# A new order for the first batch, four queries to a partition, and stores on ScalarE's queue in an attention-and-MLP kernel

## The chip, the cores and the metric

The kernel runs on one core of one Trainium2 chip. The metric is device time in microseconds (us), lower is better. Engines are named as in the profile: PE is TensorE's matmul, PEld its weight load, DVE is VectorE, ACT is ScalarE, POOL is GpSimd, SP is SyncE, which here only issues DMAs. A name with a q behind it (SPq, ACTq) is that engine's instruction sequencer, for instance when it issues a DMA. PSUM is the memory in which PE leaves its products. "L494" is line 494 of the kernel that is being profiled.

## The reference

Eight batches of causal retention (attention without softmax, with a decay by distance), followed by a low-rank mix of tokens and an MLP, both with a residual. Inputs and outputs are float32.

```python
# q, k, v: (8 batches, 8 heads, 576 tokens, 64)
scores = q @ k^T / sqrt(64)
ret    = scores * where(i >= j, gamma[h] ** (i - j), 0)
x      = concat_heads(ret @ v)                       # (8, 576, 512)
h      = (x^T @ U @ V)^T                             # U: (576, 32), V: (32, 576)
u      = x + h
out    = u + relu(u @ w_ch1) @ w_ch2                 # w: (512, 2048), (2048, 512)
```

## The kernel before

A batch has 4.5 chunks of 128 tokens, so two batches share nine chunks, the fifth being half one batch's and half the other's. The work on one batch before its MLP is called its front: load, cast, transpose q and k (`TQ`, `TK` in the new kernel), scores (`SC`), the masked scores `ret` on DVE, values (`RV`), the scaled result `xt` on DVE, the mix (`MA`, `MH`) that gives `ut`, and `uT`. The MLP has two halves, `Y1` (ACT evicts with Relu) and `Y2` (DVE adds the residual into `o_sb`, which is stored). From batch 1 on, the front of the next batch is interleaved with the MLP of the current one.

```python
def load_chunk(p, c):                                # one chunk: q, k, v together
    t = qkv_pool.tile([P, 3, H, D], BF16, ...)
    f = stage.tile([P, 3, H, D], FP32, ...)
    for j, dram in ((1, k), (0, q), (2, v)):
        for rows, b, t0 in parts(p, c):
            nc.sync.dma_start(out=f[rows, j, :, :],  # partition = token, 256-byte pieces
                in_=dram[b, :, t0:t0 + L, :].rearrange("h s d -> s h d"))
    nc.vector.tensor_copy(out=t[:, 0:2, :, :], in_=f[:, 0:2, :, :])      # DVE: cast q, k
    nc.gpsimd.tensor_tensor(out=t[:, 2, :, :], in0=f[:, 2, :, :], ...)   # POOL: cast, scale v
# ... Y2, its last step: one store of 128 rows in order, on SP
    nc.vector.tensor_tensor(out=o_sb, in0=ps, in1=st["u", c0 + i], op=ALU.add)
    nc.sync.dma_start(out=out_flat[row0 + i * P:row0 + (i + 1) * P, :], in_=o_sb)
# ... the program: only PE, POOL and SP are in manual order, DVE and ACT are not
with tc.manual_schedule(engines={PE, POOL, SPQ}):
    ...
    interleave([], front_items(0, [], True, 0))
    load_w1(range(1, dff // W1B)); load_w2()
    for g in range(2 * NP):
        interleave(mlp_items(...), front_items(g + 1, chunks_of(g + 2)), 0.35 if g == 0 else 0.05, 0.9)
```

Of the kernel before, what the change touches and what calls it, by code (L numbers as in the profile page):

```python
# [9 lines left out]
FP32 = mybir.dt.float32  # L10
# [4 lines left out]
POOL = mybir.EngineType.Pool  # L15
SPQ = mybir.EngineType.SP
# [23 lines left out]
def kernel(  # L40
# [25 lines left out]

    XC = 4
    NCH = 9

# [5 lines left out]
    stage = ctx.enter_context(tc.tile_pool(name="stage", bufs=4))  # L75
    qkv_pool = ctx.enter_context(tc.tile_pool(name="qkv_pool", bufs=9))
    qkT_pool = ctx.enter_context(tc.tile_pool(name="qkT_pool", bufs=6))
# [5 lines left out]
    mix_pool = ctx.enter_context(tc.tile_pool(name="mix_pool", bufs=2))  # L83
# [7 lines left out]


# [3 lines left out]
    pos = consts.tile([P, NCH, H], FP32, name="pos")  # L96
    lngt = consts.tile([P, NCH, H], FP32, name="lngt")
# [3 lines left out]

# [3 lines left out]
    V_B = consts.tile([P, 5 * P], BF16, name="V_B")  # L105

    vx = [consts.tile([P, H, D], BF16, name=f"vx{i}") for i in range(2)]

    qTx = [consts.tile([P, NHP, P], BF16, name=f"qTx{i}") for i in range(2)]
    w1_sb = consts.tile([P, NCC, dff], BF16, name="w1_sb")  # L110
    w2_sb = consts.tile([P, NF, dm], BF16, name="w2_sb")

    def early_consts():
        make_identity(nc, ident)
        nc.gpsimd.memset(lnb, math.log(scale))

        nc.gpsimd.iota(
            pos[:, 0:5, :], pattern=[[P, 5], [0, H]], base=0, channel_multiplier=1,
            allow_small_or_imprecise_dtypes=True,
        )  # L120
        nc.gpsimd.iota(
            pos[:, 5:NCH, :], pattern=[[P, 4], [0, H]], base=P, channel_multiplier=1,
            allow_small_or_imprecise_dtypes=True,
        )
        nc.gpsimd.iota(
            pos[HALF:P, XC, :], pattern=[[0, H]], base=HALF, channel_multiplier=1,
            allow_small_or_imprecise_dtypes=True,
        )
        for h in range(H):
            nc.vector.memset(lngt[:, :, h], lng[h])  # L130
        nc.vector.tensor_tensor(out=lngt, in0=lngt, in1=pos, op=ALU.mult)
        nc.scalar.activation(out=vscale, in_=lngt, func=AF.Exp, bias=lnb, scale=-1.0)
        nc.scalar.activation(out=qscale, in_=lngt, func=AF.Exp, bias=0.0, scale=1.0)
        make_upper_triangular(nc, tri, val=1.0, diag=True)
        nc.vector.tensor_copy(out=trix, in_=tri)
        nc.vector.memset(trix[0:HALF, HALF:P], 0.0)
        for t in vx:
            nc.vector.memset(t[0:HALF, :, :], 0.0)
        for t in qTx:
            nc.vector.memset(t[:, :, HALF:P], 0.0)  # L140
        for t in (U_A, U_B, V_A, V_B):
            nc.vector.memset(t, 0.0)

    def load_mixer():
        nc.gpsimd.dma_start(
            out=U_A[:, 0:4, 0:R],
            in_=moe_U[0:4 * P, :].rearrange("(c p) r -> p c r", p=P),
        )
        nc.gpsimd.dma_start(out=U_A[0:HALF, 4, 0:R], in_=moe_U[4 * P:S, :])
        nc.gpsimd.dma_start(out=V_A[0:R, 0:S], in_=moe_V)  # L150
        nc.gpsimd.dma_start(out=U_B[HALF:P, 0, 0:R], in_=moe_U[0:HALF, :])
        nc.gpsimd.dma_start(
            out=U_B[:, 1:5, 0:R],
            in_=moe_U[HALF:S, :].rearrange("(c p) r -> p c r", p=P),
        )
        nc.gpsimd.dma_start(out=V_B[0:R, HALF:HALF + S], in_=moe_V)

    W1B = 512

    def load_w1(fbs):  # L160
        for fb in fbs:
            for cc in range(NCC):
                nc.gpsimd.dma_start(  # L163
                    out=w1_sb[:, cc, fb * W1B:(fb + 1) * W1B],
                    in_=moe_w_ch1[cc * P:(cc + 1) * P, fb * W1B:(fb + 1) * W1B],
                )

    def load_w2():
        for f in range(0, NF, 2):
            nc.gpsimd.dma_start(  # L170
                out=w2_sb[:, f:f + 2, :],
                in_=moe_w_ch2[f * P:(f + 2) * P, :].rearrange("(f p) d -> p f d", p=P),
            )

    def parts(p, c):

        if c < XC:
            return [(slice(0, P), 2 * p, c * P)]
        if c > XC:
            return [(slice(0, P), 2 * p + 1, c * P - 4 * P - HALF)]  # L180
        return [(slice(0, HALF), 2 * p, 4 * P), (slice(HALF, P), 2 * p + 1, 0)]


    def load_chunk(p, c):
        t = qkv_pool.tile([P, 3, H, D], BF16, tag="qkv", name="qkv")
        f = stage.tile([P, 3, H, D], FP32, tag="stage", name="stage_t")
        for j, dram in ((1, k), (0, q), (2, v)):
            for rows, b, t0 in parts(p, c):
                L = rows.stop - rows.start
                nc.sync.dma_start(  # L190
                    out=f[rows, j, :, :],
                    in_=dram[b, :, t0:t0 + L, :].rearrange("h s d -> s h d"),
                )
        nc.vector.tensor_copy(out=t[:, 0:2, :, :], in_=f[:, 0:2, :, :])  # L194
        nc.gpsimd.tensor_tensor(  # L195
            out=t[:, 2, :, :], in0=f[:, 2, :, :],
            in1=vscale[:, c, :, None].to_broadcast([P, H, D]), op=ALU.mult,
        )
        if c == XC:
            nc.gpsimd.tensor_copy(out=vx[p % 2][HALF:P, :, :], in_=t[HALF:P, 2, :, :])  # L200
        sts[p]["qkv"][c] = t


    def attention_items(p, chunks, st, pe_transpose, lag, loads):
        items = []
        qkv = st["qkv"]
        loads = list(loads)

        def T(c):
            t = qkv[c]  # L210
            qkT = qkT_pool.tile([P, 2 * NHP, P], BF16, tag="qkT", name="qkT")
            st["qkT", c] = qkT
            if not pe_transpose:
                nc.sync.dma_start_transpose(  # L214
                    out=qkT, in_=t[:, 0:2, :, :].rearrange("p j h d -> p (j h d)")
                )
                return
            pst = ps_big.tile([P, 2 * NHP, P], BF16, tag="ps_big", name="pst")
            for j in (1, 0):
                for hp in range(NHP):  # L220
                    nc.tensor.transpose(  # L221
                        pst[:, j * NHP + hp, :],
                        t[:, j, 2 * hp:2 * hp + 2, :].rearrange("p h d -> p (h d)"),
                        ident,
                    )
            nc.scalar.activation(out=qkT, in_=pst, func=AF.Copy)  # L226

        def ST(c):

            t = qkv[c]  # L230
# [4 lines left out]
            vt = vx[p % 2] if c == XC else t[:, 2, :, :]  # L235
            for hp in range(NHP):
                nc.tensor.matmul(  # L237
                    pss[:, hp, :],
                    t[:, 1, 2 * hp:2 * hp + 2, :].rearrange("p h d -> p (h d)"),
                    vt[:, 2 * hp:2 * hp + 2, :].rearrange("p h d -> p (h d)"),  # L240
                    start=(first and hp == 0), stop=True, skip_group_check=True,
                )
# [4 lines left out]
        def SC(c):  # L247

            qkT = st["qkT", c]
            psc = ps_sc.tile([P, 2, NHP, P], FP32, tag="ps_sc", name="psc")  # L250
            for hp in range(NHP):
                for hl in range(2):
                    pb = hl * HALF
                    nc.tensor.matmul(  # L254
                        psc[:, hl, hp, :],
                        qkT[pb:pb + HALF, NHP + hp, :],
                        qkT[pb:pb + HALF, hp, :],
                        start=True, stop=True,
                    )
            po = ps_o.tile([P, 2, 512], FP32, tag="ps_o", name="po")  # L260
            st["po", c] = po
            if c > 0:
                s_sb = st["s", c - 1]
                qT = qkT
                if c == XC:
                    qT = qTx[p % 2]
                    nc.gpsimd.tensor_copy(
                        out=qT[:, :, 0:HALF], in_=qkT[:, 0:NHP, 0:HALF]
                    )
                for hp in range(NHP):  # L270
                    for hl in range(2):
                        pb = hl * HALF
                        nc.tensor.matmul(
                            po[:, hl, hp * D:(hp + 1) * D],
                            qT[pb:pb + HALF, hp, :],
# [3 lines left out]
            ret = ret_pool.tile([P, H, P], BF16, tag="ret", name="ret")  # L279
            mask = trix if c == XC else tri  # L280
            nc.vector.tensor_tensor(  # L281
                out=ret.rearrange("p (hp hl) i -> p hl hp i", hl=2), in0=psc,
                in1=mask[:, None, None, :].to_broadcast([P, 2, NHP, P]),
                op=ALU.mult,
            )
            st["ret", c] = ret

        def RV(c):
            t = qkv[c]
            ret = st["ret", c]  # L290
            po = st["po", c]
            for h in range(H):
                hp, hl = h // 2, h % 2
                nc.tensor.matmul(  # L294
                    po[:, hl, hp * D:(hp + 1) * D], ret[:, h, :], t[:, 2, h, :],
                    start=(c == 0 and hp == 0), stop=True, skip_group_check=True,
                )
            xt = x_pool.tile([P, dm], BF16, tag="x", name="xt")
            st["x", c] = xt
# [219 lines left out]
```

## Time and profile before

| | before |
|---|---|
| median of the first 3 runs | 381.78 us (378.99 to 381.91) |
| span of the profiled run, granted clock | 381.3 us, 0.978 |
| first MLP matmul | 41.8 us |
| first matmul of batch 1's MLP ("MLP 1") | 93.0 us |
| from there to the end | 288.3 us |

The page of the profile, busy tenths in 40 slices of 9.5 us, shows PE full from the eleventh slice on, and the DMA engines full before that:

```profile
PE 329.2 (86%) x2440; PEld 176.1 (46%) x2440; DVE 142.9 (37%) x199; ACT 123.2 (32%) x244; POOL 62.4 (16%) x86
...
PE   2655794887997999999998989998999999999995
...
PEclk9999996799899999999999999999999999999999
DMA  9999999995995149995994279997991480040012
```

(In this kernel the throttle's first record is at 47.1 us; PEclk shows 9 before it, although a matmul of 512 columns took 427 ns there, against 216 ns later.)

In the list of PE's waits (engine, line, what it waited for; us in total, times, longest) nothing is large; all that falls after 93 us adds up to about 17 us:

```profile
PE po L294 <- DVE ret L281: 9.6, 10, 2.6
PE pst L221 <- DVE qkv L194: 7.3, 2, 5.9
PE psc L254 <- DMA qkT<-qkv: 5.7, 2, 4.6
...
PE ps_y_936 L426 <- DMA uT<-ut: 1.9, 1, 1.9
```

So there are two regimes. Up to 93 us PE is held up by loads and by the chain through the first fronts; from 93 us on it is nearly saturated and each attention piece costs its full time.

### The profile page before, as it was taken

How to read it: one execution, taken by the hardware profiler on the slowest of the kernel's cores; microseconds unless marked ns; L12 is line 12 of the kernel's file. 1: busy time of each engine (PE TensorE's matmuls, PEld its weight loads, DVE VectorE, ACT ScalarE, POOL GpSimd, SP SyncE). 2: the span in 40 equal slices, each digit the busy share in tenths (PEclk: the TensorE clock that was granted, in tenths of full speed). 3: DMA queues.
4: the chain of work that ended last, by engine and by line, in shares of the span. 5: the costliest groups of instructions: out<-in, count | busy, mean ns of one | idle time of the engine just before them, and what ended most of it. 6: DMA issues, size and time to landing. Idle time of an engine off the chain costs nothing.

```text
span 381.3 us, 5987 instructions
## 1 busy us (share of the span) xinstructions
PE 329.2 (86%) x2440; PEld 176.1 (46%) x2440; DVE 142.9 (37%) x199; ACT 123.2 (32%) x244; POOL 62.4 (16%) x86
## 2 busy tenths in 40 slices
PE   2655794887997999999998989998999999999995
PEld 1432341433673444544664435444764445447642
DVE  4454201555252342544335324552544424340021
ACT  3322361200572006501771035303660056007600
POOL 2746821221022000121021001220121000000000
PEclk9999996799899999999999999999999999999999
DMA  9999999995995149995994279997991480040012
GB/s 181 206 210 179 199 196 186 206 185 132 191 212 97 57 110 194 202 211 136 175 228 83 73 126 218 186 173 157 218 196 40 114 153 2 28 125 29 0 57 83
DMA packets 173659, 54.81 MB, mean 144 GB/s; under 512 B 164864, under 2 KB 169024, under 8 KB 173632
## 3 DMA queue, kind: packets, MB, share of 16 engines
q1 hardware_dynamic: 167840, 50.09, 73.6%
q0 software_dynamic: 5792, 4.34, 7.5%
q8 instruction: 19, 0.31, 0.4%
q14 instruction: 8, 0.07, 0.1%
HBM read 37.00 MB, written 9.44 MB: 122 GB/s over the span
## 4 chain that ended last, share of the span: by engine, by line
PE 56%; DMA 18%; SPq 13%; DVE 6%; issue 3%; ACT 2%; POOL 1%; DVEq 0%; POOLq 0%
DMA stage_t<-in_q_dram 8%; SPq L190 7%; DMA uT<-ut 4%; SPq L214 4%; DMA stage_t<-in_v_dram 3%; DVE ret L281 3%; PE po L294 2%; PE psc L254 2%; PE psa L361 2%; PE ph L379 1%; SPq L390 1%; DVE o_sb L443 1%; DVE qkv L194 1%; DMA qkT<-qkv 1%; DMA U_A<-in_moe_U_dram 1%
## 5 line engine op out<-in xcount | busy, mean ns | idle before, releaser
L426 PEld LDWEIGHTS <-w_sb 128*128 128x128 bf16 x768 | 72.2, 100 | 55.9 <-issue 17.3
L195 POOL TENSOR_TENSOR qkv<-stage_t,vscale 128x512 bf16<-128x512 f32 x36 | 38.1, 1060 | 216.2 <-DMA stage_t<-in_v_dram 156.0
L281 DVE TENSOR_TENSOR ret<-psc,tri 128x1024 bf16<-128x1024 f32 x32 | 39.1, 1223 | 50.9 <-PE psc L254 50.9
L194 DVE CAST qkv<-stage_t 128x1024 bf16<-128x1024 f32 x36 | 25.8, 718 | 64.4 <-DMA stage_t<-in_q_dram 64.4
L300 DVE TENSOR_TENSOR xt<-po,qscale 128x512 bf16<-128x512 f32 x36 | 24.8, 689 | 17.6 <-PE po L294 17.5
L366 ACT ACTIVATE a_sb<-psa 128x512 bf16<-128x512 f32 x8 | 4.8, 597 | 80.5 <-PE psa L361 76.5
L385 DVE TENSOR_TENSOR ut<-ph,xt 128x512 bf16<-128x512 f32 x36 | 24.6, 689 | 14.5 <-PE ph L379 14.4
L294 PE MATMUL po<-qkv,ret 128*128 128x64 bf16 x288 | 15.6, 201 | 9.6 <-DVE ret L281 9.6
L254 PE MATMUL psc<-qkT 64*128 64x128 bf16 x288 | 16.0, 238 | 8.8 <-DMA qkT<-qkv 5.7
L294 PEld LDWEIGHTS <-ret 128*128 128x128 bf16 x288 | 13.5, 103 | 19.6 <-DVE ret L281 15.1
L244 ACT ACTIVATE s_sb<-pss 128x512 bf16<-128x512 f32 x32 | 19.0, 593 | 5.4 <-PE pss L237 5.4
L254 PEld LDWEIGHTS <-qkT 64*128 64x128 bf16 x288 | 9.1, 102 | 22.3 <-issue 10.1
L237 PEld LDWEIGHTS <-qkv 128*128 128x128 bf16 x128 | 10.5, 105 | 6.9 <-issue 1.9
L237 PE MATMUL pss<-qkv 128*128 128x128 bf16 x112 | 12.0, 235 | 1.8 <-ACT s_sb L244 1.0
L437 PEld LDWEIGHTS <-y_3686 128*128 128x128 bf16 x80 | 7.8, 98 | 9.3
L437 PEld LDWEIGHTS <-y_929 128*128 128x128 bf16 x80 | 7.8, 101 | 9.3 <-issue 1.1
L437 PEld LDWEIGHTS <-y_1861 128*128 128x128 bf16 x80 | 7.6, 98 | 8.6
L437 PEld LDWEIGHTS <-y_2793 128*128 128x128 bf16 x80 | 7.6, 98 | 8.6
L221 PE MATMUL pst<-ident,qkv 128*128 128x128 bf16 x40 | 5.2, 311 | 7.3 <-DVE qkv L194 7.3
L226 ACT ACTIVATE qkT<-pst 128x1024 bf16<-128x1024 bf16 x5 | 5.1, 1024 | 15.1 <-PE pst L221 15.1
L163 POOL DMA_DIRECT2D w_sb<-in_moe_w_ch_dram x16 | 9.3, 597 | 3.5 <-DMA w_sb<-in_moe_w_ch_dram 3.5
L437 PEld LDWEIGHTS <-y_1457 128*128 128x128 bf16 x64 | 6.1, 98 | 7.1
(522 smaller groups left out, 536.7 us busy)
## 6 DMA issues: line engine op xcount, KB each, us to landing
out_dram<-o_sb SPq DMA_DIRECT2D x36, 256.0 KB, 2.2
stage_t<-in_k_dram SPq DMA_DIRECT2D x32, 256.0 KB, 3.9
stage_t<-in_q_dram SPq DMA_DIRECT2D x32, 256.0 KB, 5.1
stage_t<-in_v_dram SPq DMA_DIRECT2D x32, 256.0 KB, 5.1
w_sb<-in_moe_w_ch_dram POOLq DMA_DIRECT2D x16, 128.0 KB, 7.2
w_sb<-in_moe_w_ch_dram POOLq DMA_DIRECT2D x8, 256.0 KB, 11.5
stage_t<-in_k_dram SPq DMA_DIRECT2D x8, 128.0 KB, 4.8
stage_t<-in_q_dram SPq DMA_DIRECT2D x8, 128.0 KB, 4.8
```

Of the source, the lines that this page charges most:

```text
L190: nc.sync.dma_start(out=f[rows, j, :, :], in_=dram[b, :, t0:t0 + L, :].rearrange("h s d -> s h d"),)
L194: nc.vector.tensor_copy(out=t[:, 0:2, :, :], in_=f[:, 0:2, :, :])
L195: nc.gpsimd.tensor_tensor(out=t[:, 2, :, :], in0=f[:, 2, :, :], in1=vscale[:, c, :, None].to_broadcast([P, H, D]), op=ALU.mult,)
L237: nc.tensor.matmul(pss[:, hp, :], t[:, 1, 2 * hp:2 * hp + 2, :].rearrange("p h d -> p (h d)"), vt[:, 2 * hp:2 * hp + 2, :].rearrange("p h ...
L244: nc.scalar.activation(out=s_sb, in_=pss, func=AF.Copy)
L254: nc.tensor.matmul(psc[:, hl, hp, :], qkT[pb:pb + HALF, NHP + hp, :], qkT[pb:pb + HALF, hp, :], start=True, stop=True,)
L281: nc.vector.tensor_tensor(out=ret.rearrange("p (hp hl) i -> p hl hp i", hl=2), in0=psc, in1=mask[:, None, None, :].to_broadcast([P, 2, NHP ...
L294: nc.tensor.matmul(po[:, hl, hp * D:(hp + 1) * D], ret[:, h, :], t[:, 2, h, :], start=(c == 0 and hp == 0), stop=True, skip_group_check=True,)
L300: nc.vector.tensor_tensor(out=xt.rearrange("p (hp hl d) -> p hl hp d", hl=2, d=D), in0=po[:, :, 0:NHP * D].rearrange("p hl (hp d) -> p hl ...
L385: nc.vector.tensor_tensor(out=ut, in0=ph, in1=st["x", c], op=ALU.add)
L426: nc.tensor.matmul(ps[:, 0:n], w1_sb[:, cc, f * P:(f + 1) * P], uT[:, cc, t0:t0 + n], start=(cc == 0), stop=(cc == NCC - 1),)
L437: nc.tensor.matmul(ps, st["y1"][:, f, i * P:(i + 1) * P], w2_sb[:, f, :], start=(f == 0), stop=(f == NF - 1),)
```

## The change

The intent: shorten the 93 us before the steady part. The first batch's front gets one hand-written order on all engines; queries come in one wide load with four consecutive tokens to a partition (1 KB pieces instead of 256 B); the weights come in eight loads of 512 KB instead of 24 smaller ones; and output stores move to ACT's queue, so that they can't hold up loads on SP. The diff, cut to its core:

```diff
-    def load_chunk(p, c):
-        ... k, q, v of 128 tokens; cast of q and k; scaling of v
+    def load_q(g, quick=False):                      # all 512 tokens of a batch, 1 MB
+        f = stage.tile([P, H, J, D], FP32, tag="q_f", name="q_f", bufs=1)          # J = 4
+        i = nc.sync.dma_start(
+            out=f, in_=q[g, :, t0:t0 + 4 * P, :].rearrange("h (p j) d -> p h j d", j=J))
+        ... cast_q: DVE, four casts
+    def load_kv(g, m, cast=True): ...                # k, v per chunk; cast_kv: DVE and POOL
+    def load_x(p, part=None, cast=True): ...         # the shared chunk 4
...
-                nc.sync.dma_start_transpose(out=qkT, in_=t[:, 0:2, :, :]...)       # 128 rows
+                nc.sync.dma_start_transpose(         # 32 rows: chunk m, columns in order (j i)
+                    out=qT[:, m].rearrange("p hp (j i) -> p (hp j) i", j=J),
+                    in_=t[m * PJ:(m + 1) * PJ].rearrange("p hp j hl d -> p (hp j hl d)"))
...
-                nc.sync.dma_start(
-                    out=out_flat[row0 + i * P:row0 + (i + 1) * P, :], in_=o_sb
-                )
+                nc.scalar.dma_start(                 # partition (j p) holds row (p j)
+                    out=dst.rearrange("(p j) d -> j p d", j=J),
+                    in_=o_sb,
+                )
...
-    with tc.manual_schedule(engines={PE, POOL, SPQ}):
-        ... interleave([], front_items(0, [], True, 0)) ...
+    with tc.manual_schedule(engines={PE, POOL, SPQ}):
+        with tc.manual_schedule(engines={DVE, ACT}):
+            load_q(0, quick=True); ... first, w1_last = first_front()   # uT formed in PSUM
+        i = load_q(1)                                # after the first weights
+        ...
+        interleave(mlp.y1_items(), fill, LEAD[0], LEAD[1])  # Y1 of batch 0 with front 1's start
+        i = load_q(2)
+        for f in range(NF):                          # Y2 of batch 0, after front 1
+            for i in range(3):
+                mlp.Y2(i, f, 1)
+        mlp.Y2(3, 0, NF)
+        ... then MLPs 1 to 7, each front at 65% of the MLP before (SKEW = 0.65)
```

Because a partition holds four consecutive queries, a chunk's result row `(p j)` sits on partition `(j p)`. The store must undo this, and its destination pattern is `[4, 32, 512]`.

## The prediction

> **What bounds the kernel now.** Two regimes. From about 93 us on, TensorE bounds it: the timeline shows four 512-column matmuls each 0.86 us (216 ns apiece), each attention piece inserted at its full cost, and 94% PE busy from 100 to 360 us (window table). All PE waits listed after 93 us add up to about 16 us: transposed u (DMA uT, 7.4), masked scores (DVE ret, 4.9), a_sb (ACT, 2.1), small rest. Before 93 us TensorE does only about 42 us of full-clock work (MLP 0, 27.6 us; two fronts, about 14 us). The first MLP matmul starts at 41.8 us; until 46.8 us a 512-column matmul takes about 427 ns, twice the later value. The Trainium skill ("TensorE: Matmul & The Clock Gate", the HAM clock gate) says an idle array runs at half clock; the trace agrees. DMA is saturated: busy in every slice to 90 us, about 200 GB/s, 164,864 of 173,659 packets under 512 B. From 40 to 60 us the weights hold 82% of the DMA time; the k/q/v loads then take about 21 us to land and the first transposes 9.9 us. PE waits 4.65 us for qkT, falls to clock 0.54 and finishes MLP 0 only at 93 us.
>
> **What the change does.**
> 1. Front 0: q comes as one 1 MB load of 1 KB packets instead of 256 B ones; only 64 of chunk 4's tokens are loaded; U and V need no slow queue; the chunks are software-pipelined; uT is formed in PSUM by 16 transposes plus 4 matmuls instead of four serial matmul, DVE, PE, ACT rounds (1.8 us each). At the trace's 214 GB/s the 3.6 MB land by about 18 us; DVE (cast 0.36, mask 1.23, scale 0.69 us per chunk) is next. First MLP matmul: 28.5 us (range 25 to 33), 13 us earlier. No dummy matmuls: the clock is still half there.
> 2. Weights: four wide loads per matrix, started after the first loads (about 19 us) and needing about 3.6 us each (software queue: 7.5% of the span = 28.6 us for both matrices). Y1 follows to about 44 us.
> 3. Given back: most of front 1 now runs alone on PE between Y1 and Y2 (instruction order), with 80 more PE transposes, and its last k/v pair shares DMA with w2, which itself waits for two earlier pairs. I estimate that pair at 58 us, front 1 done at 68, Y2 13.8 us more: MLP 1 starts at 81 us (74 to 88) against 93.
> 4. Steady part: fronts finish at 65% of the preceding MLP, so uT and a_sb waits vanish; stores no longer block loads on SP (114 us of SP waiting for o_sb). Gain 10 of the 16 us. 288 us becomes 278.
>
> DMA transposes are split (32-row q, 128-row k), and stores cost ACT some issue time (0.34 us each); I expect both off the critical path.
>
> **Prediction.** 81 + 278 = 359, rounded to 358 us; 8 in 10 between 346 and 370. Faster by over 2%: 0.92; same: 0.06; slower: 0.02.
>
> **What would show it.** First MLP matmul near 28 us; MLP 1's first near 81; PE idle on k/v loads or w2 between 45 and 65; no uT wait over 0.5 us after that; DMA packets near 140,000; last MLP still about 34 us.
>
> **What would make it wrong.** The 32-row transposes may be slow and hold SP's queue, so fronts starve in the steady part (355 becomes 370+). w2 may land much earlier, or front 1's chain take less than 3 us a chunk (345). DVE's strided q casts may be slow. ACT, waiting in order for o_sb, may delay the Relu evictions.

## More of the kernel before

The queues and issues (last column: median us from issue to landing) show that a store of a chunk's 256 KB was done 2.2 us after issue:

```profile
q1 hardware_dynamic: 167840, 50.09, 73.6%
...
out_dram<-o_sb SPq DMA_DIRECT2D x36, 256.0 KB, 2.2
...
stage_t<-in_q_dram SPq DMA_DIRECT2D x32, 256.0 KB, 5.1
```

## The result

The changed kernel is correct and takes 439.98 us (median of 4 runs, 438.06 to 441.71), against 381.23 us for the kernel before in the same rounds. The ratio is 1.155 (95% interval 1.147 to 1.163): slower by 15%. Ratios here are the mean time of one kernel's fast runs over that of the other's in the same rounds, so not quite the ratio of the medians.

| profiled run | predicted | before | after |
|---|---|---|---|
| first MLP matmul | 28.5 us | 41.8 | 29.0 |
| first matmul of MLP 1 | 81 us | 93.0 | 95.2 |
| from there to the end | 278 us | 288.3 | 344.3 |

The first matmuls of the first MLP and of MLP 1, in PE's timeline of the changed kernel (start, duration):

```profile
29.02 1.22 PE L651 MATMUL ps_y_559<-uT,w_sb 128*128 128x512 bf16 x4
...
95.17 0.71 PE L651 MATMUL ps_y_1085<-uT,w_sb 128*128 128x320 bf16 x4
```

PE's row of the page now has holes in the part that was full, and the clock falls there (439.5 us span, clock 0.905):

```profile
PE 342.9 (78%) x2487; PEld 185.6 (42%) x2520; DVE 154.2 (35%) x246; ACT 131.3 (30%) x257; POOL 55.1 (13%) x83
...
PE   1777664877799469983799955896669999999993
...
PEclk9999665996899888995899998799689999999997
DMA  6999999936933969979940999529994374051012
```

PE's waits answer to the list above: the waits on `uT` are gone, of those on transposed q and k 0.7 us is left, and one on `xt` has come, 40 us, with three on `o_sb`:

```profile
PE po L465 <- DVE xt L494: 40.3, 12, 8.0
PE po L486 <- DVE ret L474: 10.4, 10, 2.1
...
PE ph L532 <- DVE ut L538: 5.7, 1, 5.7
PE ps_y_3124 L651 <- DVE o_sb L669: 3.8, 1, 3.8
PE ps_y_2176 L651 <- DVE o_sb L669: 2.9, 1, 2.9
PE ps_y_1097 L651 <- DVE o_sb L669: 2.8, 1, 2.8
```

Queues: the stores have a queue of their own, q10. It takes 7.6% of the time of 16 engines for the 9.44 MB of output. Of the 36 stores, 32 have the permuted pattern; the four of the shared chunks write 128 rows in order. For stores and for the loads of q, k and v, the page gives no time from issue to landing in this kernel:

```profile
q1 hardware_dynamic: 132880, 39.17, 60.0%
q10 hardware_dynamic: 4800, 9.44, 7.6%
q0 software_dynamic: 4224, 4.19, 6.1%
...
out_dram<-o_sb ACTq DMA_DIRECT2D x36, 256.0 KB
```

So the first MLP matmul came when it was predicted. MLP 1 did not start earlier than before, and 56 us were lost after its start.

### The profile page after: what moved, and what is told of

Its sections match the earlier page's. It is cut to its first block, busy times and chain, and to the rows that moved or that the text cites. A ratio compares the mean times of both kernels' runs of the same rounds, so it can differ in the third digit from the quotient of the medians.

```text
span 439.5 us, 6173 instructions
## 1 busy us (share of the span) xinstructions
PE 342.9 (78%) x2487; PEld 185.6 (42%) x2520; DVE 154.2 (35%) x246; ACT 131.3 (30%) x257; POOL 55.1 (13%) x83
## 3 DMA queue, kind: packets, MB, share of 16 engines
q10 hardware_dynamic: 4800, 9.44, 7.6%
HBM read 36.92 MB, written 9.44 MB: 105 GB/s over the span
## 4 chain that ended last, share of the span: by engine, by line
PE 48%; DMA 25%; SPq 16%; DVE 5%; issue 2%; POOL 1%; ACT 1%; ACTq 0%; DVEq 0%; POOLq 0%
DMA kv_f<-in_k_dram 9%; SPq L283 6%; DMA w_sb<-in_moe_w_ch_dram 5%; DMA q_f<-in_q_dram 4%; SPq L388 3%; SPq L364 2%; DMA kT<-kv 2%; DMA out_dram<-o_sb 2%; PE psa L515 2%; DMA kv_f<-in_v_dram 1%; DVE o_sb L669 1%; PE ph L532 1%; SPq L306 1%; PE po L486 1%; PE psc L449 1%
## 5 line engine op out<-in xcount | busy, mean ns | idle before, releaser
L273 POOL TENSOR_TENSOR kv<-kv_f,vscale 128x512 bf16<-128x512 f32 x32 | 34.0, 1066 | 259.9 <-DMA kv_f<-in_v_dram 195.9
L465 PE MATMUL po<-s_sb,qT 64*128 64x64 bf16 x224 | 9.0, 206 | 40.1 <-DVE xt L494 40.1
L295 DVE CAST kv<-kv_f 128x512 bf16<-128x512 f32 x32 | 16.3, 514 | 60.8 <-DMA kv_f<-in_k_dram 60.0
L494 DVE TENSOR_TENSOR xt<-po,qscale 128x512 bf16<-128x512 f32 (+1 forms) x37 | 25.5, 688 | 26.9 <-PE po L486 26.7
L269 DVE CAST q_bf<-q_f 128x512 bf16<-128x512 f32 x30 | 11.7, 448 | 44.6 <-DMA q_f<-in_q_dram 44.6
L486 PE MATMUL po<-kv,ret 128*128 128x64 bf16 x256 | 14.2, 203 | 9.2 <-DVE ret L474 9.0
L449 PE MATMUL psc<-qT,kT 64*128 64x128 bf16 x256 | 13.8, 232 | 1.0 <-DMA kT<-kv 0.7
L428 PE MATMUL pss<-kv 128*128 128x128 bf16 x112 | 12.5, 242 | 2.4 <-POOL kv L273 1.3
L428 PEld LDWEIGHTS <-kv 128*128 128x128 bf16 x112 | 9.5, 110 | 7.5 <-issue 2.1
L449 PEld LDWEIGHTS <-kT 64*128 64x128 bf16 x256 | 7.8, 99 | 11.2 <-issue 8.3
```

What stands on the lines that cost most here:

```text
L273: nc.gpsimd.tensor_tensor(out=dst[rows], in0=src[rows], in1=vscale[rows, c, :, None].to_broadcast([n, H, D]), op=ALU.mult,)
L295: nc.vector.tensor_copy(out=t[:, 0], in_=f[:, 0])
L428: nc.tensor.matmul(pss[:, hp, :], pair_cols(st["k", c], hp), pair_cols(vt, hp), start=(first and hp == 0), stop=True, skip_group_check=True,)
L449: nc.tensor.matmul(psc[0:n, hl, hp, 0:n], kT[pb:pb + HALF, hp, 0:n], qTv[pb:pb + HALF, hp, 0:n], start=True, stop=True,)
L486: nc.tensor.matmul(po[0:n, hl, hp * D:(hp + 1) * D], ret[:, h, 0:n], vt[:, h, :], start=((c == 0 or not cross) and hp == 0), stop=True, sk ...
L494: nc.vector.tensor_tensor(out=st["x", c][rows].rearrange("p (hp hl d) -> p hl hp d", hl=2, d=D), in0=po[rows, :, 0:NHP * D].rearrange("p h ...
```

## The experiments

Six theories were tested. They have letters in the expectations:

- **S**: the store's destination has an outermost dimension of 4, which confines it to few DMA engines; stores are slow, and loads behind them land late.
- **D**: VectorE runs in order, and its automatic order puts casts of loads that have not landed ahead of `xt`, `ret` and `o_sb`, for which PE waits.
- **A**: ACT, running in order, waits for a store's data or a slow issue, ahead of the Relu evictions for which PE waits.
- **T**: the 32-row query transposes are slow.
- **Q**: (later) transposes wait on SP's queue behind stores and loads.
- **F**: (later) front 1, alone on PE, leaves gaps that `Y2` of batch 0 could fill.

For S there is a page to lean on. The Trainium skill, "DMA: Bandwidth & Descriptors", section "Why a DMA increments its semaphore by 16 and not by 1", says that a DMA uses the largest number of engines, at most 16, that divides the slowest dimension on both sides; the row "Use all 16 engines" in its section "Rules for kernel authors" tells to put a multiple of 16, ideally the 128 partitions, outermost. By that, `[4, 32, 512]` is moved by 4 engines. The trace agrees. In the quiet tail, where only stores move, the engines of the kernel before are 8 to 9 tenths busy while a store runs, at 388 to 396 GB/s in its fullest slices (372 to 381.3 us, in 40 slices):

```profile
DMA  8980000000000019970000000000029960000000
GB/s 335 388 344 18 0 0 0 0 0 0 0 0 0 0 62 396 361 308 0 0 0 0 0 0 0 0 0 0 0 106 388 396 238 0 0 0 0 0 0 0
```

In the changed kernel they are two tenths busy (a 2 is 20 to 29%, and 4 of 16 are 25%), at 97 to 109 GB/s (426 to 439.5 us):

```profile
DMA  2222241121222224112122222501222222200000
GB/s 97 97 97 109 97 61 12 49 73 73 97 103 103 109 97 61 12 49 73 67 103 97 109 97 85 79 12 30 67 61 97 103 109 103 79 36 0 0 0 0
```

The packed trace also has the completion semaphores, the counters by which DMAs report that they have landed. In the changed kernel each of the 32 permuted stores raises its semaphore in 5 steps, one early and four at the end, which fits four engines, and has landed 5.8 to 12.8 us after its issue (median 7.3); the four stores of rows in order, on the same queue, do so in 16 steps and land after 2.0 to 2.7 us. The tail, from the end of the last `o_sb` on DVE to the end of the span, grows from 3.3 us to 7.0 us.

Timed runs of one launch on one core have no state ("unknown"), so effects under about 3% of single runs are not read below. The kernel before, run beside them, was 377.8 to 386.9 us; three of these runs, of 384.8 us and more, were slow.

### First call: one suspect at a time, from the changed kernel

**e1_store16.** Four stores of 32 partitions each, still permuted and still on ACT: no DMA is confined to four engines, but there are four times as many issues.

```diff
-                nc.scalar.dma_start(out=dst.rearrange("(p j) d -> j p d", j=J), in_=o_sb)
+                dj = dst.rearrange("(p j) d -> j p d", j=J)
+                for j in range(J):
+                    nc.scalar.dma_start(out=dj[j], in_=o_sb[j * PJ:(j + 1) * PJ, :])
```

> Edit: every permuted store becomes four stores of 32 partitions each, so that no store has an outermost dimension of 4. Stores should then move at about 390 GB/s as in the kernel before (the changed kernel's last store moves at about 100 GB/s). Theory D (VectorE waits, in order, for casts of late q/k loads and holds up scores and outputs behind them): only the tail after the last matmul shrinks, 7 to about 4 us, time 430 to 438 us. Theory S (four-engine stores clog the DMA and make loads late): q loads land in 4 to 6 us instead of 10, TensorE waits for xt fall by more than half, time under 400 us. Theory T (32-row transposes clog the DMA): as D.

Measured: 407.14 us, 33 less than the changed kernel's 439.98, though not under the 400 that S forecast. The wait on `xt` falls from 40.3 to 22.1 us. A new wait appears, 14.1 us on ACT's evictions; ACT's timeline shows its largest part, 16 store issues in a row that hold the next Relu eviction back to 105.74 (the issues alone are 6.6 us of the 12.71, the rest are gaps between them):

```profile
92.99 12.71 ACTq L679 DMA_DIRECT2D out_dram<-o_sb  x16
105.74 1.09 ACT L655 ACTIVATE y<-ps_y 128x320 bf16<-128x320 f32 x3 [23.22 <-DMA kT<-kv]
```

**e2_qt128.** The queries transposed in 128-row blocks of 1024 columns, twice per batch, and put into chunk order by ACT.

```diff
-                nc.sync.dma_start_transpose(out=qT[:, m]..., in_=t[m * PJ:(m + 1) * PJ]...)
+                if m < 2:
+                    h2 = slice(2 * m, 2 * m + 2)
+                    nc.sync.dma_start_transpose(out=self.q2[:, h2]..., in_=t[:, h2]...)
+                    self.copy(qT[:, :, h2]..., self.q2[:, h2]...)          # ACT
```

> Edit: in the steady part q goes through two DMA transposes of 128 rows x 1024 columns per batch, the shape that the kernel before used, into a temporary, and ScalarE copies it into place, instead of four transposes of 32 rows x 2048. Theory T: the DMA throughput in full slices rises from about 60-110 to about 200 GB/s, loads land in half the time, 385 to 405 us. Theories D and S: 430 to 442 us, TensorE's wait for xt stays at 30 to 45 us.

Measured: 448.21 us, 8 more, and the wait on `xt` stays at 35.5 us, as D and S say (the time is above their range). So T found no support; e10 below, which keeps the 32-row transposes and takes 387.76 us, rules it out as the main cause. This run also adds copies on ACT and takes one `q_bf` buffer away, so it does not say what the transposes cost by themselves.

**e3_castpool.** The casts of q, k and the shared chunk from DVE to POOL (batch 0's stay, `quick`).

```diff
-            else:
+            elif quick:
                 nc.vector.tensor_copy(out=dst, in_=src)
+            else:
+                nc.gpsimd.tensor_copy(out=dst, in_=src)
...
-        nc.vector.tensor_copy(out=t[:, 0], in_=f[:, 0])
+        (nc.gpsimd if g else nc.vector).tensor_copy(out=t[:, 0], in_=f[:, 0])
```

> Edit: the casts of q, k and the boundary chunk for batches 1 to 7 move from VectorE to GpSimd; loads, stores and transposes stay. Theory D: VectorE no longer waits for a DMA, TensorE's waits for xt (40 us) and o_sb (10 us) fall under 10 us in sum, MLP 1 starts at about 86 us instead of 95, time 370 to 390 us. Theories S and T: the data stay late, so TensorE waits for transposed q and k instead of xt, time 420 to 440 us.

Measured: 422.78 us, 17 less. PE's wait on `xt` is 1.7 us, so D holds for that wait. But PE now waits 21.5 us for ACT's evictions, 12.4 for `kT`, and 8.3 for a small copy (`qTx`) that stands behind the casts on POOL. With S still there, more than half of the 38.6 us that this wait lost comes back as other waits. MLP 1 starts at 84.9 us, 10 earlier than in the changed kernel and near the 86 that D forecast, but the time is in the range that was expected of S and T.

**e5_early.** Each batch's loads are issued one front earlier, into the staging buffers that the casts have just freed; there are no more buffers than before. The casts stay on DVE in their old places.

```diff
-        out = [(load_q, g)] + [(load_kv, g, m) for m in range(4)]
+        out = [(load_q, g, False, False)] + [(load_kv, g, m, False) for m in range(4)]
...
-            items = fronts[g].items(loads_of(g + 1), nxt=fronts.get(g + 1))
+            items = fronts[g].items(both(g + 1), nxt=fronts.get(g + 1))   # casts g+1, loads g+2
```

> Edit: the loads of a batch are issued one whole front earlier, each into the buffer that the cast just emitted has freed; the casts stay on VectorE in the front where they were. Same bytes, same DMA shapes. Theory D: the data are there when VectorE comes to the cast, its waits for k and q loads fall from 105 us to under 30, time 375 to 400 us. Theories S and T: DMA stays clogged, 420 us or more.

Measured: 436.77 us, which is not apart from the changed kernel's. DVE waited 9.1 us for q loads (44.6 in the changed kernel) but still 57.1 us for k loads (60.0): issuing them earlier in the program did not make them land before the casts. This is a weak test of D, because a k load still cannot start before a cast has freed its buffer.

### Second call: the queue of the stores

**e6_storesp.** The four-engine stores, on SP instead of ACT (`nc.scalar.dma_start` becomes `nc.sync.dma_start` in the store).

> Edit: the changed kernel with its stores back on SP's queue, shape unchanged (outermost dimension 4). If what hurts is that ScalarE waits in order for o_sb and for the issue of the stores (theory A), TensorE's waits for Relu evictions vanish and the time falls to 405 to 420 us. If it is the four-engine stores themselves (theory S), the loads stay late and it stays at 425 to 445 us.

Measured: 443.62 us. The queue alone changes nothing that can be read, so A is not what costs the changed kernel its 59 us; the slow stores do their harm from either queue.

**e7_store16sp.** The stores split in four (as e1), on SP.

> Edit: stores in four pieces of 32 partitions (as e1, 407 us) and on SP's queue. Theory A: the 14 us in which TensorE waited for Relu evictions in e1 go, 390 to 397 us. If only the four-engine shape mattered: 403 to 410 us as e1. Theory D says in both cases that VectorE still waits about 75 us for q and k loads and TensorE about 20 us for xt.

Measured: 407.36 us, as e1. Its waits differ: PE waits 15.0 us for `qTx` on POOL, 13.4 for `xt`, 7.2 for `kT`. Split stores are worth 33 us on ACT's queue and 36 on SP's.

**e8_combo_sp** and **e9_combo_act.** Both have split stores, the casts on POOL (as e3), and the `qTx` copy on DVE. In e8 the stores are on SP, in e9 on ACT.

```diff
-                    nc.gpsimd.tensor_copy(
+                    nc.vector.tensor_copy(
                         out=qTv[:, :, 0:HALF], in_=st["xT"][:, 0, :, 0:HALF]
                     )
```

> Edit: e7 and e3 together (16-engine stores on SP, casts of batches 1 to 7 on GpSimd), and the small boundary copy of q (qTx), for which TensorE waited 8 us in e3 because GpSimd had loads to wait for, on VectorE. If S, A and D are the causes and add up (33, about 10 and 17 us, and 8 us): 358 to 372 us, below the kernel before. If a fourth cause is left, e.g. 32-row transposes: over 378 us, with TensorE waiting for transposed q or k.

> Edit: as e8 but the 16-engine stores stay on ScalarE's queue. Theory A: 5 to 15 us slower than e8, with TensorE waiting for Relu evictions. If the queue makes no difference once loads do not hold VectorE: within 3 us of e8.

Measured: e8 381.49 us, e9 403.68 us. S, D and the queue together give back the whole loss: e8 equals the kernel before (379.76 beside it). It is not in the 358 to 372 us expected if the causes simply added up. With S and D out of the way, A is worth 22 us. The causes hide one another: with stores on ACT, D is worth 3 us (e9 against e1), which can't be read; with stores on SP, 26 (e8 against e7). PE's largest wait in e9:

```profile
PE ps_y L653 <- ACT y L657: 28.1, 6, 9.7
```

and the place of its longest part, in ACT's timeline: eleven store issues stretch over 11.78 us, and Relu evictions that were due stand behind them:

```profile
87.86 11.78 ACTq L681 DMA_DIRECT2D out_dram<-o_sb  x11
99.69 1.10 ACT L657 ACTIVATE y<-ps_y 128x320 bf16<-128x320 f32 x3 [28.16 <-DMA qT<-q_bf]
```

The issues alone are 4.0 us of it. For about 7 us ACT waited until earlier DMAs had landed that had the same completion semaphore, most of them transposes and a load on SP's queue; over all of e9 such waits ahead of stores come to about 60 us on ACT (in the packed trace; e10 below shows the same on SP). So A is for the greater part such a wait, and not the time of issue.

The Trainium skill, "DMA: Bandwidth & Descriptors", section "Issuing engines are not separate DMA queues", says that issuing from several engines saves only the sequencer's time to initiate DMAs. That agrees with e6 (no gain). That section does not say what e9 shows: that on an engine which also computes, issues and the waits ahead of them block the computing.

What was left in e8 was a wait for `kT`, and SP's timeline shows sixteen store issues in front of the transposes:

```profile
PE psc L451 <- DMA kT<-kv: 12.3, 3, 6.5
```

```profile
87.19 7.72 SPq L681 DMA_DIRECT2D out_dram<-o_sb  x16
...
95.54 1.33 SPq L366 DMA_TRANSPOSE qT<-q_bf  x1
...
99.85 1.21 SPq L390 DMA_TRANSPOSE kT<-kv  x1
```

### Third call: the shape alone, and two repairs

e1 changes the shape and the number of stores at once. **e10_wrongrows** changes the shape alone. Its result is wrong: each store writes 128 whole rows in natural order, so the rows are permuted.

```diff
-                nc.scalar.dma_start(out=dst.rearrange("(p j) d -> j p d", j=J), in_=o_sb)
+                nc.scalar.dma_start(out=dst, in_=o_sb)
```

> The changed kernel, but each store writes its 128 partitions to 128 rows in natural order, so the destination's outermost dimension is 128 and not 4; the number of stores, their bytes, their queue and their place stay. The result is wrong on purpose (rows permuted). Theory S (the four-row shape of the store confines it to few DMA engines and delays the loads behind): 395 to 410 us, as with the stores split in four. Rival (it was the order or queue of the stores): 432 to 442 us.

Measured: 387.76 us, 52 less than the changed kernel, and below the range expected of S. So the shape of the store accounts for nearly all of the loss against before, and splitting it in four paid about 19 us of that back (407 against 388; four times the issues, and the waits that come with them). With 128 outermost, a store on ACT's queue lands after 2.7 us and the query load after 6.5:

```profile
q10 hardware_dynamic: 5184, 9.44, 7.6%
...
out_dram<-o_sb ACTq DMA_DIRECT2D x36, 256.0 KB, 2.7
q_f<-in_q_dram SPq DMA_DIRECT2D x8, 1024.0 KB, 6.5
```

MLP 1 starts at 95.2 us in both kernels, and the difference from there on is 344.3 against 290.8 us. The trace shows how it arises right after. DVE's timeline of the changed kernel, which begins with the last residual add of batch 0:

```profile
98.52 0.69 DVE L669 TENSOR_TENSOR o_sb<-ps_y_1064,ut 128x512 f32<-128x512 f32 x1 [5.66 <-DMA out_dram<-o_sb]
99.13 1.42 DVE L269 CAST q_bf<-q_f 128x512 bf16<-128x512 f32 x4
109.32 0.43 DVE L295 CAST kv<-kv_f 128x512 bf16<-128x512 f32 x1 [8.77 <-DMA kv_f<-in_k_dram]
109.67 1.22 DVE L474 TENSOR_TENSOR ret<-psc,tri 128x1024 bf16<-128x1024 f32 x1
```

and of e10:

```profile
95.40 0.69 DVE L669 TENSOR_TENSOR o_sb<-ps_y,ut 128x512 f32<-128x512 f32 x1 [2.51 <-PE ps_y L661]
96.00 1.42 DVE L269 CAST q_bf<-q_f 128x512 bf16<-128x512 f32 x4
100.02 0.43 DVE L295 CAST kv<-kv_f 128x512 bf16<-128x512 f32 x1 [2.59 <-DMA kv_f<-in_k_dram]
100.36 1.22 DVE L474 TENSOR_TENSOR ret<-psc,tri 128x1024 bf16<-128x1024 f32 x1
```

In the changed kernel VectorE was idle for 5.66 us before the add, at the end for an `o_sb` buffer, that is, for an earlier store to land (`<-DMA out_dram<-o_sb`). PE had finished the product at 95.33, so the buffer cost about 3 us of this; in e10 the add waited only for PE. VectorE then casts q. The next cast is of a k load of batch 3, a batch ahead of the scores that PE is working on; the load was issued at 104.03 in one kernel and at 96.30 in the other (SP's timeline), DVE waited for it 8.77 us against 2.59, and `ret`, which PE needs, stands behind that cast: 109.67 against 100.36. From issue to the start of its cast the load took 5.3 us against 3.7. So of the 9.3 us by which `ret` comes later here, 7.7 are a later issue and 1.6 a slower load.

SP's list of waits shows why the load was issued late. Although the stores are on ACT's queue, SP stood still until a store had landed, ahead of the `kT` transpose at 98.48 and again ahead of this load:

```profile
SPq L388 <- DMA out_dram<-o_sb: 9.3, 1, 9.3
SPq L283 <- DMA out_dram<-o_sb: 4.3, 1, 4.3
```

In e10 the two waits are 4.4 and 1.2 us. The operands in the packed trace give the link: in these programs the DMAs of SP and ACT share eight completion semaphores, and a DMA is issued only when the last one on its semaphore has landed. The transpose has the semaphore of the store issued at 91.70, the load that of the store at 93.95; these took 6.7 and 10.0 us to land, in e10 2.1 and 3.3. So a slow transfer on one queue holds back the other queue.

These are the first 9 of the 53.5 us; the later fronts were not followed one by one. SP has no further wait of this kind before the program's end, and the loads themselves are slower there: after 95 us q loads landed in 10.1 us (median of four) against 6.6 in e10, and the longest k load took 10.0 us against 8.0. VectorE waited 60.0 us for k loads and 44.6 for q loads in the whole run, against 30.1 and 33.6 in e10.

That loads are slower because the stores fill four engines is an inference, since the profile shows no single DMA engine: if q10's 7.6% of sixteen engines sits on four of them, it is 30.4% there, and 60.0 + 30.4 + 6.1 = 96.5% of those four engines' span is taken (an estimate from the queue table and from the page's rule; it takes the other queues as evenly spread). It is no measure of how full they are, since packet times of different queues overlap: from 70 to 80 us the share of all sixteen is 139%.

**e11_y2mix.** e8, with the second weight products of batch 0 spread over the second half of front 1.

```diff
-        interleave(mlp.y1_items(), fill, LEAD[0], LEAD[1])
+        ... cut = the first 45% of fill, by cost
+        interleave(mlp.y1_items(), fill[:cut], LEAD[0], LEAD[1])
...
-        for f in range(NF):
-            for i in range(3):
-                mlp.Y2(i, f, 1)
-        mlp.Y2(3, 0, NF)
+        interleave(mlp.y2_items(), fill[cut:], 0.05, 1.0)
```

> The combination with stores on SP, with the second weight products of batch 0 spread over the second half of front 1, instead of after it. Theory F (front 1 alone leaves PE idle between its chunks, which the products can fill): MLP 1 starts at 80 to 85 us instead of 90.7, and the time falls from 381.5 to 369 to 374. Rival (front 1 is bound by its loads and PE's work pushes it out): MLP 1 still after 88 us, time 378 or more.

Measured: 374.55 us; MLP 1 starts at 80.6 us instead of 90.7. F holds for MLP 1's start. Of the ten microseconds seven remain in the time, too few to be read from single runs: PE then waits once 9.6 us for `kT`.

**e12_sporder.** e8, with batch 2's first transposes placed before batch 0's stores on SP, and the next q load after the current chunks' first transposes.

```diff
-            next_load()                              # before the front's first transposes
+            if pe:                                   # steady fronts: after them
+                next_load()
...
+        front2 = Front(2, False)                     # ahead of Y2 of batch 0 and its stores
+        front2.begin(lambda c, fn, *a: fn(*a), 0)
+        front2.begin(lambda c, fn, *a: fn(*a), 1)
```

> The combination with stores on SP, with the first transposes of batch 2 issued on SP before batch 0's stores, and the next q load issued after the transposes of the current chunk. Theory Q (PE's 12.3 us of waiting for kT came from transposes issued behind stores and loads on one queue): kT waits below 4 us, 369 to 375 us. Rival (they wait for a busy DMA, whatever the order): kT waits 9 us or more, 378 to 384.

Measured: 364.26 us, and the wait for `kT` fell from 12.3 to 2.5 us. Q holds; the run gained 17 us on e8, 7 more than that wait lost, and was faster than the range expected. The two edits were not run apart.

**e13_both.** e11 and e12 together, timed.

> Both edits, Y2 in front 1 and the order on SP. If both theories hold and add up: 358 to 366 us, below the kernel before by 4 to 6%. If neither: 378 to 384.

Measured: 372.52 us (370.03 to 373.22, ratio to before 0.976, interval 0.965 to 0.986): a miss, slower than e12 alone. MLP 1 does start at 82.1 us, but PE then stands still for 8.3 us. The chain, in SP's, DVE's and PE's timelines:

```profile
76.98 1.71 SPq L308 DMA_DIRECT2D x_f<-in_k_dram  x2
...
85.67 1.20 SPq L390 DMA_TRANSPOSE kT<-kv  x1
86.97 7.95 SPq L682 DMA_DIRECT2D out_dram<-o_sb  x16
```

```profile
90.36 0.69 DVE L672 TENSOR_TENSOR o_sb<-ps_y,ut 128x512 f32<-128x512 f32 x1 [8.70 <-DMA out_dram<-o_sb]
```

```profile
91.11 5.76 PE L654 MATMUL ps_y<-uT,w_sb 128*128 128x320 bf16 x24 [8.32 <-DVE o_sb L672]
```

The fourth residual add needs one of three `o_sb` buffers. The stores of the first three had been ready earlier, since `Y2` was earlier, but stood on SP behind the loads and transposes that now come first, until 86.97. The next matmul of `Y1` waits for the PSUM bank that this add frees. More `o_sb` buffers would take this wait away, but a fourth does not fit (a buffer takes 2 KB of a partition, and 6.4 KB were left for all of them), so this was not tried.

### Fourth call: the permutation undone, and the best version timed

**e14_nat.** The changed kernel with queries in natural rows: four loads of 128 tokens with 256-byte pieces, 128-row transposes, one natural 128-row store on ACT. Unlike e10 it is correct.

```diff
-        i = nc.sync.dma_start(
-            out=f, in_=q[g, :, t0:t0 + 4 * P, :].rearrange("h (p j) d -> p h j d", j=J))
+        for m in range(4):
+            i = nc.sync.dma_start(out=f[:, :, m],
+                in_=q[g, :, t0 + m * P:t0 + (m + 1) * P, :].rearrange("h s d -> s h d"))
...
-                nc.scalar.dma_start(out=dst.rearrange("(p j) d -> j p d", j=J), in_=o_sb)
+                nc.scalar.dma_start(out=dst, in_=o_sb)
```

(with the masks, scales, U and V in natural order too)

> The changed kernel with the queries in natural rows: loaded as four 128-token loads of 256-byte pieces, transposed in 128-row blocks, and stored as 128 whole rows on ScalarE's queue. A correct kernel, so this is the direct undo of one part of the change. Theory S (the shape of the store is what the permutation costs): 383 to 396 us, near the 387.8 of the run with rows stored in the wrong order. Rival (the wide query load was worth its price): 405 us or more.

Measured: 387.06 us. Undoing the permutation alone, in a correct kernel, takes 53 us away, as e10 did. The first MLP matmul is at 29.8 us instead of 29.0. No gain of the wide load in the first front can be read from this: in e6, which has the first front of the changed kernel, that matmul is at 32.3 us.

**e15_nat_sp** and **e17_nat_act.** Natural rows with all the other repairs (casts on POOL, `qTx` on DVE, e12's order on SP), stores on SP and on ACT.

> Natural query rows, whole stores on SP, casts on POOL, and the SP order of the run that gave 364.3. One store issue where there were four, four query loads where there was one. If SP's issue time is what still delays the transposes: 352 to 361 us. If not: 362 to 368.

> The same with the stores on ScalarE's queue. Theory A (ScalarE blocks on a store wait or a slow issue, before the Relu evictions that PE needs): at least 10 us slower than with the stores on SP. Rival (it was the sixteen small issues per batch that blocked ScalarE, and whole stores cost nothing there): within 4 us of it.

Measured: e15 370.01 us (367.84 to 373.15, ratio to before 0.974, interval 0.965 to 0.984), e17 380.05. e15 is a miss by a little: fewer store issues, but four query loads instead of one, did not beat e12: its timed runs are 6 us slower than those of e12b below. So once the stores are split and in a good order, the permuted layout is ahead, by 1.6%; the two kernels differ in loads, transposes and stores at once, and which of these makes the difference was not tried. Stores on ACT cost 10 us here, against 22 when they were split; one run of e17 lies outside the range of four of e15, so A seems to hold for whole stores too, at half the size. In e17's trace PE waits 5.3 us for ACT's evictions, and 16.0 for `ret` (4.5 in e15), which was not traced to ACT.

**e12b_again.** The same kernel as e12, timed.

> The very kernel that gave 364.3 us, timed: 361 to 368, ratio to the kernel before 0.945 to 0.965. If that run was a lucky one: 370 or more.

Measured: 364.01 us (362.38 to 366.50), ratio to the kernel before 0.957 (interval 0.949 to 0.965). It beats both kernels, and it is correct. PE's largest waits in it:

```profile
PE psq L375 <- DVE q_bf L269: 9.0, 1, 9.0
...
PE psc L451 <- DMA kT<-kv: 2.9, 3, 1.3
```

MLP 1 starts at 88.5 us and the rest takes 275.2 us.

| run | time, us | MLP 1 starts | from there on | what it shows |
|---|---|---|---|---|
| before | 381.2 | 93.0 | 288.3 | |
| after | 440.0 | 95.2 | 344.3 | |
| e10, store shape alone (wrong rows) | 387.8 | 95.2 | 290.8 | S: 52 us |
| e14, natural rows | 387.1 | 97.6 | 287.6 | S, in a correct kernel |
| e8, split stores on SP, casts on POOL | 381.5 | 90.7 | 289.0 | S, D and the queue |
| e12b, with SP's order | 364.0 | 88.5 | 275.2 | and Q |

## Why the prediction was wrong

The prediction was 358 us (346 to 370) with 0.92 on faster; measured were 440 us, slower. Of these 82 us, about 66 came after the start of MLP 1 (step 4 below) and 14 before it (step 3).

1. *"First MLP matmul: 28.5 us."* Right: 29.0 us, 12.7 earlier than before. That it was met to half a microsecond is luck, for e6 with the same first front has 32.3. That *"the clock is still half there"* was not so: from 30.1 us on the matmuls of 512 columns took 216 ns each, half of the 427 ns before.

2. *"Y1 follows to about 44 us."* Wrong by 10 us, in a small way: the weights did not hold it up, and 13 of Y1's 16 steps were done by 40.6 us, but the last three stand behind pieces of the fronts in PE's order, and Y1 ended at 53.8.

3. *"MLP 1 starts at 81 us (74 to 88)."* Wrong by 14 us: 95.2. The sum in the prediction was 68 us for the end of front 1 plus 13.8 us of Y2. Front 1 ended at about 80 us. Until then PE waited for DVE, not for the weights: 5.7 us for `ut`, which on DVE stood behind the cast of a late load, 3.7 us for `xt`, which stood behind the cast of the *next* batch's queries, and 4.3 us for `ret`. PE was busy 6.75 us of the 12 from 58 to 70 us, at a clock of 0.54. The Trainium skill, "TensorE: Matmul & The Clock Gate", section "Part 1: The HAM clock gate", says that a gate sets PE's clock by how busy PE has been; this stretch agrees. Casts on POOL alone brought MLP 1 forward by 10 us (e3, 84.9), with the other edits of e8 by 4.5, and filling the gaps with Y2 brought it forward by 10 more (e11 against e8). The prediction had named this order ("front 1 alone on PE") and set its price too low.

4. *"Gain 10 of the 16 us. 288 us becomes 278."* This is the step that failed: 344 us, 66 us off. The sentence behind it was *"DMA transposes are split …, and stores cost ACT some issue time (0.34 us each); I expect both off the critical path."* The prediction costed the stores by the time of their issue on ACT and never costed the transfer. The diff shows `"(p j) d -> j p d"` with j = 4; the transfer runs at about a quarter of the rate and lands after 7.3 us (median) instead of 2.0 to 2.7. It was not off the critical path: with its shape alone put right the same kernel takes 291 us there (e10), and 53 of the 66 us are gone. DVE's wait for k loads halves with it (60.0 to 30.1 us). The predicted end of the `uT` waits did come. The predicted 278 us were reached too, at 275 (e12b), but only after the stores, the casts on DVE and the order on SP were repaired.

5. *"stores no longer block loads on SP (114 us of SP waiting for o_sb)."* Not shown to be worth anything: with the same stores on SP instead of ACT the time was the same while S held (443.6 and 440.0), and with S mended SP was the better queue by 22 us (e8 against e9) and by 10 (e15 against e17). So these runs give no sign that the 114 us that SP waited in the kernel before held it up.

6. Of the list of what would make it wrong: *"The 32-row transposes may be slow"* did not show in e2, nor in e10 against e14. *"DVE's strided q casts may be slow"*: the casts themselves took 0.45 us each on average; it was their place in an in-order engine, before a load had landed, that cost (e3). *"ACT, waiting in order for o_sb, may delay the Relu evictions"* was right about the delay, worth 10 to 22 us but hidden while S held; in e9 ACT waited mostly for the completion semaphores of other DMAs, not for `o_sb`. The store's shape was not on the list.

What stays open: how the 52 us of the slow stores divide between the `o_sb` buffers, the late issues behind shared completion semaphores and the slower loads, because more buffers did not fit and no run separated the semaphores; how much of e12's gain belongs to which of its two edits; and the cost of the 32-row transposes by themselves.

## What to carry to other kernels

When a change permutes a layout, look at the pattern of every DMA that undoes it: a store with an outermost dimension of 4 costs the rest of the kernel far more than its own length, and here it lost 52 us, where no gain of the wide load could be read in the first front. Look at which DMAs share a completion semaphore: a slow transfer on one queue can hold back issues on another. Issue stores from an engine that computes nothing on the critical path, and put on that queue first what the next stage waits for. A cast placed automatically on an in-order engine waits for its load ahead of everything behind it; give casts of late loads to an engine that has nothing urgent.

## What the Trainium skill lacked or had wrong

- "DMA: Bandwidth & Descriptors", "Why a DMA increments its semaphore by 16 and not by 1" and "Rules for kernel authors": the rule on the outermost dimension agrees with the trace (97 to 109 GB/s against 388 to 396 for 256 KB stores). The page does not say what such a DMA does to the rest of a kernel: with only 8.4 of 53.2 MB moved so (32 stores of 256 KB), 52 of 440 us were lost (e10 against after).
- The same page, "Issuing engines are not separate DMA queues": it speaks only of issue time saved. Lacking is what it costs when the issuing engine also computes, and waits, in order, ahead of its own compute: 22 us with 64 KB stores (e9 against e8), 10 us with 256 KB stores (e17 against e15), and 12.71 us for sixteen issues in a row on ACT (e1), 6.6 of them issue time.
- The same page: beyond its general row on coalescing small transfers, it has no figure for what it costs to split a confined store so that it reaches all engines. Here the split cost about 19 us of the 52 (e1 against e10).
